# One kernel of attention and token/channel mixing: an earlier load of the second token weight, a third staging buffer, and GpSimd masks for batch 1

## Chip, cores and metric

The kernel runs on one core of a Trainium2 chip. The metric is the device time of one launch in microseconds (us). Engines are named as in the profile: PE (TensorE, matrix products), DVE (VectorE), ACT (ScalarE), POOL (GpSimd), and SP (SyncE, which here only issues DMAs; its rows are marked SPq).

## What is computed

```
scores = q k^T / 8 + min(-(cum_i - cum_j), 0), causal;  cum = cumsum(max(s, 0))
attn   = softmax(scores) v                       8 batches, 8 heads, 576 positions, 64 wide
x      = attn, heads side by side                (8, 576, 512)
u      = x + (relu(x^T w_tok1) w_tok2)^T         w_tok1 576x256, w_tok2 256x576
out    = u + relu(u w_ch1) w_ch2                 w_ch1 512x1536, w_ch2 1536x512
```

All inputs and the output are float32 in device memory; the kernel computes in bf16.

## The kernel before

Work is cut by batch, and inside a batch by "quads" of four heads. One quad is: load k and q (two DMAs of 576 KB, L680), cast them to bf16 (L699 to L703 by POOL, DVE or ACT), transpose them (DVE, L714), scores on PE (L759) in two phases of 16 and 24 matmuls into four psum banks, one exponential a head and phase on ACT (L776), the causal mask, and attention times v on PE (L803, nine matmuls a head, called AV below), then a reciprocal and a normalisation on DVE (L812, L817; ACT L823 for some heads of batch 0). Only two neighbouring blocks of 128 keys are kept for a row of queries; a flag computed at run time sends other inputs to the function `general`, which does not run here. v arrives in chunks of 128 rows (L635) and is multiplied by decay weights (L647, by POOL or DVE) before AV can read it.

The mask is made in one of two ways. Where `pem` is true (all of batch 0, and heads 4 to 7 of batch 1) PE adds a matrix of large negative numbers to the scores: L747 before the scores in batch 0, L769 after them in batch 1. Elsewhere POOL sets the masked half of the exponentials to zero afterwards (L784, `affine_select`), one instruction for the diagonal block of four heads, five a quad: two for the first phase and three for the second.

The token mix of batch 0 (`tok0`) goes by four groups m of two heads: x times w_tok1 (L923, ten matmuls), a transposed copy of x (L936, four), then w_tok2 (L942, two), evicted as uT. `chan0` follows with channel weight 1 (L965, 48 matmuls of 512 columns) and channel weight 2 (L988 and L992). Batches 1 to 7 use `tok` (L1028, L1036, L1053, L1057, and L1083 for a transposition by PE) and `chan` (L1111, L1137).

Weights come in float32 and need a staging buffer until they are cast. w_tok2 is staged in a tile of the ring `x`. The four groups of channel weight 1 and the four of weight 2 are staged in the two halves of the tile `ga` (columns 0 and 1536) and in one of the two tiles `vf`, which later hold v. All DMAs are issued by SP in one order.

The order of all instructions on all engines is not written by hand. Each piece of work is an `op` of `Plan` with its engines, costs and what it reads and writes; `once` lays the ops out by list scheduling (PE, SP and POOL take the lowest `prio` that is ready, the others the longest tail), and `run` repeats this 5 + 60 times with slightly shaken tails and keeps the shortest plan. The kernel is then emitted in that order, and each engine runs its instructions strictly in order. `fills` puts matmuls on zeros (L1264) where the plan leaves PE idle in the first 45 us. `load_op` chains the loads: two loads keep the order in which the code names them, while stores may go between.

The order of the loads is set at the end of the function (L1159 to L1199): k and q of batch 0, v for heads 0 to 3 (five chunks), w_tok1, v for heads 4 to 7 (five chunks), w_tok2, the four groups of channel weight 1, then batch 1 with channel weight 2 between its parts.

Of the kernel before, what the change touches and what calls it, by code (L numbers as in the profile page):

```python
# [9 lines left out]
FP32 = mybir.dt.float32  # L10
# [39 lines left out]
RING = 2048  # L50


class Plan:
# [103 lines left out]
    def run(self, passes=5, search=60):  # L157
        best = None
        self.lengths = []
        rng = random.Random(1)  # L160
        base = None
        for i in range(passes + search):
            self.reset()
            if i >= passes:
                for o in self.ops:
                    o.tail = base[o] + (rng.gauss(0.0, 2.0) if rng.random() < 0.02 else 0.0)
            used = {o: o.tail for o in self.ops} if i else None
            order, length = self.once(i > 0)
            if best is None or length <= best[0]:
                best = (length, [(o, o.start, o.fin, o.eng, o.fn) for o in order],  # L170
                        [(b, b.slot, b.begin, b.end) for o in order for b in o.bufs],
                        {r: list(r.uses) for o in order for b in o.bufs for r in (b.ring,)})
                base = used
            self.lengths.append(round(length, 1))
            if i < passes:
                self.tails(order)
                if base is None:
                    base = {o: o.tail for o in self.ops}
        self.length = best[0]
        for o, o.start, o.fin, o.eng, o.fn in best[1]:  # L180
            pass
        for b, b.slot, b.begin, b.end in best[2]:
            pass
        for r, u in best[3].items():
            r.uses = u
        return [o for o, *_ in best[1]]
# [276 lines left out]
def kernel(  # L463
# [28 lines left out]
    PMASK = 1  # L492
    VUS = 1.05
# [122 lines left out]
    pre = s_sb  # L616
# [22 lines left out]
    def stage_v(b, part=None):  # L639
# [30 lines left out]
        if b:  # L670
            return todo
# [60 lines left out]
    def quad(b, h):  # L732
        np_ = (b * H + h) / 2 if b else -3.0 + h / 8
        kT, qT, E = qkt[(b, h, 0)], qkt[(b, h, 1)], Buf(r_E)
        pem = b < PMASK or b == 1 and h > 0
        for ph, blocks in enumerate(PHASES):
# [13 lines left out]
            if b == 0:  # L750
                P.op({"PE": (mocc, mocc + 0.3, mask)}, reads=["neg"], writes=[(p, 1) for p in ps], prio=(np_, 0),
                     ready=(7.6, 9.3)[ph] if h == 0 else 0.0)

            def mm(ps=ps, cols=cols):
                for (jc, a, z, c0) in cols:
                    for qq in range(DQ):
                        for e in range(HQ):
                            p0 = e * TP
                            nc.tensor.matmul(out=ps[e].t[:, c0 : c0 + z - a],  # L759
                                             lhsT=kT.t[p0 : p0 + TP, jc * 128 : jc * 128 + 128, qq],  # L760
                                             rhs=qT.t[p0 : p0 + TP, a:z, qq],
                                             start=(qq == 0 and b > 0 and (not pem or c0 == 0)),
                                             stop=(qq == DQ - 1 and (not pem or b == 0 and jc == cols[-1][0])),
                                             tile_position=(p0, 0))
                if pem and b:
                    for e in range(HQ):
                        for (jc, a, z, c0) in cols:
                            n = min(128, S - jc * 128)
                            nc.tensor.matmul(out=ps[e].t[:, c0 : c0 + n], lhsT=ident[:, :], rhs=neg[:, 0:n],  # L769
                                             start=False, stop=(jc == cols[-1][0]))  # L770
            occ = (0.06 * len(cols) * HQ if pem and b else 0.0) + 0.15 + DQ * sum(c_pe(z - a)[0] + 0.01 for (_, a, z, _) in cols)
            P.op({"PE": (occ, occ + 0.3, mm)}, reads=[(kT, 0), (qT, 0)] + ([(p, 1) for p in ps] if b == 0 else ["neg"] if pem else []),
# [19 lines left out]
        for hh in range(HQ):  # L792
            pa, rc = Buf(r_sc if b < 2 else r_mx, False), Buf(r_rc, False)
# [372 lines left out]
    stage_v(0, 1)  # L1166
# [5 lines left out]
    load_tok2(Buf(r_x))  # L1172
    sga, sv = Buf(r_ga), Buf(r_vf)
# [3 lines left out]
    load_ch1(sga, 0, 3)  # L1177
    stage_qk(1, 0)
    load_ch2(sga, 1536, 0)
    stage_qk(1, HQ)  # L1180
    load_ch2(sv, 0, 1)
    load_ch2(sga, 0, 2)
    v1 = stage_v(1)
    v1[0]()
    v1[1]()
# [3 lines left out]
    load_ch2(sga, 1536, 3)  # L1189
# [13 lines left out]
    for b in range(B):  # L1203
# [8 lines left out]
    P.op({"DVE": (1.3, 1.6, lambda: nc.vector.tensor_tensor_scan(  # L1212
        out=pre[:, :], data0=one_sb[:, :].to_broadcast([64, S]), data1=wn[:, 0:S], initial=0.0, op0=ALU.mult, op1=ALU.add))},
        reads=["wn", ("sq", 10)], writes=["pre"], prio=50)

    def gaps():
        for i in range(3):
            j = 128 * (i + 1)
            nc.vector.scalar_tensor_tensor(out=gap[:, i : i + 1], in0=wn[:, j + 128 : j + 129], scalar=4.8e-7,
                                           in1=pre[:, j - 1 : j], op0=ALU.mult, op1=ALU.is_lt)  # L1220
        nc.vector.tensor_scalar(out=gap[:, 3:4], in0=cum[:, S - 1 : S], scalar1=160.0, scalar2=None, op0=ALU.is_gt)
        nc.vector.tensor_copy(out=bad[0:64, 0:4], in_=gap[:, :])
# [90 lines left out]
```

## Time and profile before

| what | value |
|---|---|
| median of 6 runs | 291.28 us (290.33 to 292.32) |
| the profiled execution | 291.42 us |
| its span in the profile | 289.7 us, so 1.72 us lie around it |
| granted PE clock, mean | 0.998 |
| PE busy | 278.0 us, 2544 matmuls |
| DVE, ACT, POOL busy | 174.9, 187.3, 91.9 us |

The profile shows one execution. A row of a timeline gives the start in us, the duration of the group in us, the engine, the line, the operation, the tiles (written <- read), the shape and the count; in square brackets stands the idle time of the engine before it and what ended it. The durations of matmuls overlap, so what a run of matmuls costs is read from its start to the start of the next.

### The profile page before, as it was taken

The numbers are of one execution on the slowest core, as the hardware profiler recorded it, in microseconds if no ns is written. First come the engines' busy times: TensorE is split into PE (matmuls) and PEld (weight loads), VectorE is DVE, ScalarE is ACT, GpSimd is POOL, SyncE is SP. The second block draws the span as 40 slices with busy tenths as digits, with TensorE's granted clock in tenths as the row PEclk, the third lists the DMA queues.
The fourth block names the chain that finished last, engine by engine and source line by source line (L and its number), as shares of the span: only waits on it lengthen the run. The fifth ranks groups of instructions, "written<-read, shape, count | busy, mean of one in ns | idle before, by whom it ended". The sixth has DMA issues, their size and how long they took to land.

```text
span 289.7 us, 6564 instructions
## 1 busy us (share of the span) xinstructions
PE 278.0 (96%) x2544; PEld 155.5 (54%) x2574; DVE 174.9 (60%) x333; ACT 187.3 (65%) x354; POOL 91.9 (32%) x143
## 2 busy tenths in 40 slices
PE   8889999998999999999999999999999999999994
PEld 3665455455754545456754545456744545357543
DVE  4963885988999765596359585785245513640022
ACT  3876876998899468986894478857842264018500
POOL 4753022637538417731282104621212102000000
PEclk9999999999999999999999999999999999999999
DMA  7999999998649999899964965951005410170032
GB/s 234 290 290 352 405 303 316 300 276 239 164 130 308 172 339 291 253 202 231 275 158 91 308 214 165 289 146 38 2 0 78 142 38 0 54 147 36 2 106 80
DMA packets 68128, 54.07 MB, mean 187 GB/s; under 512 B 53760, under 2 KB 56640, under 8 KB 68096
## 3 DMA queue, kind: packets, MB, share of 16 engines
q1 hardware_dynamic: 68096, 53.64, 66.1%
q8 instruction: 21, 0.34, 0.6%
q14 instruction: 11, 0.09, 0.1%
HBM read 40.65 MB, written 9.44 MB: 173 GB/s over the span
## 4 chain that ended last, share of the span: by engine, by line
PE 83%; SPq 5%; DMA 5%; DVE 3%; issue 2%; ACT 1%; DVEq 0%; ACTq 0%
PE pmx L1137 29%; PE pmx L1111 27%; PE psc L759 5%; PE pmx L803 5%; SPq L635 4%; PE pmx L1028 4%; PE pmx L965 4%; PE pmx L1053 4%; PE pmx L988 3%; DMA qkf<-in_q_dram 3%; DMA x<-in_moe_w_tok_dram 2%; PE psc L923 1%; DVE qkb L701 1%; PE pmx L1036 1%; SPq L680 1%
## 5 line engine op out<-in xcount | busy, mean ns | idle before, releaser
L776 ACT ACTIVATE E<-psc 128x512 bf16<-128x512 f32 x120 | 63.6, 601 | 26.4 <-PE psc L759 23.8
L784 POOL TENSOR_SCALAR_AFFINE_SELECT E<-E 128x512 bf16<-128x512 bf16 (+1 forms) x65 | 37.8, 609 | 99.7 <-ACT E L776 77.8
L1111 PEld LDWEIGHTS <-wc 128*128 128x128 bf16 x528 | 50.7, 98 | 32.1 <-issue 1.0
L1137 PE MATMUL pmx<-wc,gb 128*128 128x512 bf16 (+1 forms) x244 | 53.8, 369 | 0.5
L1111 PE MATMUL pmx<-uTb,wc 128*128 128x320 bf16 x384 | 54.2, 300 | 0.0
L1117 ACT ACTIVATE gb<-pmx 128x320 bf16<-128x320 f32 x80 | 34.5, 442 | 23.6 <-PE pmx L1111 17.7
L647 POOL TENSOR_TENSOR vp<-vf,wT 128x512 bf16<-128x512 f32 (+2 forms) x35 | 35.2, 1023 | 17.4 <-DMA vf<-in_v_dram 12.2
L685 ACT ACTIVATE junk<-qkf 128x1152 bf16<-128x1152 f32 x32 | 37.5, 1172 | 3.9 <-DMA qkf<-in_k_dram 3.7
L1137 PEld LDWEIGHTS <-gb 128*128 128x128 bf16 x252 | 23.7, 98 | 25.5 <-issue 0.9
L1137 PE MATMUL pmx<-wc,ga 128*128 128x512 bf16 x137 | 32.9, 380 | 0.4
L1111 PE MATMUL pmx<-uTa,wc 128*128 128x512 bf16 x141 | 31.8, 380 | 0.2
L803 PEld LDWEIGHTS <-E 128*128 128x128 bf16 x576 | 20.9, 97 | 6.4 <-issue 2.1
L817 DVE TENSOR_TENSOR x<-pmx,rc 128x320 bf16<-128x320 f32 x48 | 23.1, 489 | 1.4
L1117 ACT ACTIVATE ga<-pmx 128x512 bf16<-128x512 f32 x27 | 16.1, 597 | 11.6 <-PE pmx L1111 11.6
L1145 DVE TENSOR_TENSOR of<-pmx,ub 128x512 f32<-128x512 f32 (+1 forms) x17 | 11.2, 658 | 20.0 <-PE pmx L1137 17.0
L714 DVE STREAM_TRANSPOSE kT<-qkb 128x576 f32<-128x576 f32 x16 | 20.1, 1254 | 3.4 <-PE psc L759 2.3
L1137 PEld LDWEIGHTS <-ga 128*128 128x128 bf16 x144 | 13.1, 98 | 15.5 <-issue 1.5
L759 PE MATMUL psc<-qT,kT 32*128 32x256 bf16 (+2 forms) x592 | 19.1, 251 | 1.9 <-DVE qT L714 1.8
L714 DVE STREAM_TRANSPOSE qT<-qkb 128x576 f32<-128x576 f32 x16 | 19.9, 1244 | 0.4 <-POOL qkb L699 0.3
L701 DVE CAST qkb<-qkf 128x1152 bf16<-128x1152 f32 (+1 forms) x22 | 16.5, 763 | 4.9 <-DMA qkf<-in_k_dram 3.0
L759 PEld LDWEIGHTS <-kT 32*128 32x128 bf16 x640 | 13.7, 92 | 10.3 <-issue 8.1
L812 DVE RECIPROCAL rc<-pmx 128x5 f32<-128x5 f32 x48 | 8.7, 184 | 14.3 <-PE pmx L803 13.7
(115 smaller groups left out, 294.0 us busy)
## 6 DMA issues: line engine op xcount, KB each, us to landing
qkf<-in_k_dram SPq DMA_DIRECT2D x20, 576.0 KB, 6.1
qkf<-in_q_dram SPq DMA_DIRECT2D x20, 576.0 KB, 6.5
out_dram<-of SPq DMA_DIRECT2D x31, 256.0 KB, 2.4
vf<-in_v_dram SPq DMA_DIRECT2D x28, 256.0 KB, 5.9
ga<-in_moe_w_ch_dram SPq DMA_DIRECT2D x6, 768.0 KB, 7.2
vf<-in_v_dram SPq DMA_DIRECT2D x15, 128.0 KB, 5.1
vf<-in_moe_w_ch_dram SPq DMA_DIRECT2D x2, 768.0 KB, 9.9
out_dram<-of SPq DMA_DIRECT2D x10, 128.0 KB, 2.4
```

The costliest lines, as they stand in the source:

```text
L647: eng.tensor_tensor(out=vp.t[0:n, c, h0:h1, 0:D], in0=vf.t[0:n, c, h0:h1, :], in1=wT[0:n, c, b * H + h0 : b * H + h1].unsqueeze(2).to_broa ...
L685: P.op({"ACT": (1.1, 1.5, lambda: nc.scalar.activation(out=junk[:, :], in_=f.t[:, :], func=AF.Square, accum_out=sq[:, col : col + 1]))}, r ...
L701: nc.vector.tensor_copy(out=o.t[:, a:z], in_=i.t[:, a:z])
L714: nc.vector.transpose(out=T.t[:, 0:S, :].rearrange("p s q -> p (s q)").bitcast(FP32).rearrange("p (t r) -> p r t", r=R), in_=t1.t[:, :].bi ...
L759: nc.tensor.matmul(out=ps[e].t[:, c0 : c0 + z - a], lhsT=kT.t[p0 : p0 + TP, jc * 128 : jc * 128 + 128, qq], rhs=qT.t[p0 : p0 + TP, a:z, qq ...
L776: nc.scalar.activation(out=E.t[:, e, ph * 512 : ph * 512 + 512], in_=p.t[:, :], func=AF.Exp, scale=0.125)
L784: nc.gpsimd.affine_select(out=w, in_=w, compare_op=ALU.is_ge, fill=0.0, base=0, pattern=[[0, HQ], [1, n]], channel_multiplier=-1)
L803: nc.tensor.matmul(out=o[:, ic, 0 : D + 1], lhsT=E.t[:, hh, d0 : d0 + 128], rhs=vp.t[:, jc, h + hh, 0 : D + 1], start=(jc == j_lo), stop=( ...
L817: nc.vector.tensor_tensor(out=x.t[:, :, (h + hh) * D : (h + hh + 1) * D], in0=o[:, :, 0:D], in1=rc.t[:, :].unsqueeze(2).to_broadcast([128, ...
L1111: nc.tensor.matmul(out=pm.t[:, 0 : e - a], lhsT=wc1[:, m, cc * 128 : cc * 128 + 128], rhs=uT.t[:, m, a:e], start=(m == 0), stop=(m == NMC ...
L1117: lambda cc=cc, pm=pm, a=a, e=e: nc.scalar.activation(out=g.t[:, cc, a:e], in_=pm.t[:, 0 : e - a], func=AF.Relu),
L1137: nc.tensor.matmul(out=pm.t[:, na:nb], lhsT=g.t[:, cc, c * 128 : c * 128 + 128], rhs=wc2[:, cc, na:nb], start=(cc == 0), stop=(cc == NCC - 1))
```

## The change

1. `Plan.run` searches 100 times instead of 60, and besides the tails it now shakes the priorities of whole groups of PE work (`moved`); a plan that gets stuck is skipped.
2. `pem` holds for batch 0 alone: heads 4 to 7 of batch 1 are masked by POOL (L784) and the block of L769 is gone.
3. `w_tok2` is loaded after the second of the five v chunks for heads 4 to 7 of batch 0, no longer after the fifth.
4. A second tile of the ring `vf` stages channel weights: group 3 of weight 1 goes to it (before: to the first half of `ga`), and the groups of weight 2 take `ga` 0, `ga` 1536, `vf` and `ga` 0. Group 2 of weight 2 is loaded after the first v chunk of batch 1, no longer ahead of all of them.
5. The AV results of heads 4 to 7 of batch 0 go to the psum ring `pmx` instead of `psc`.
6. `pre` is a tile of its own, [64, 3], filled by a reduction over three blocks and two additions instead of a running sum over 576 columns in the tile of `s`.

```diff
-    def run(self, passes=5, search=60):
+    def run(self, passes=5, search=100):
...
             if i >= passes:
+                mode = rng.random()
                 for o in self.ops:
-                    o.tail = base[o] + (rng.gauss(0.0, 2.0) if rng.random() < 0.02 else 0.0)
+                    o.tail = base[o] + (rng.gauss(0.0, 2.0) if mode < 0.7 and rng.random() < 0.02 else 0.0)
+                trial = dict(moved)
+                if mode > 0.4:
+                    for g in sorted({p[0] for p in ranks.values()}):
+                        if rng.random() < 0.1:
+                            trial[g] = trial.get(g, 0.0) + rng.gauss(0.0, 0.7)
+                for o, p in ranks.items():
+                    o.prio = (p[0] + trial.get(p[0], 0.0),) + p[1:]
...
-    pre = s_sb
+    pre = sb("pre", [64, 3], FP32, fast)
...
-        if b:
+        if b or part and LATER:
             return todo
...
-        pem = b < PMASK or b == 1 and h > 0
+        pem = b < PMASK
...
-                if pem and b:
-                    for e in range(HQ):
-                        for (jc, a, z, c0) in cols:
-                            n = min(128, S - jc * 128)
-                            nc.tensor.matmul(out=ps[e].t[:, c0 : c0 + n], lhsT=ident[:, :], rhs=neg[:, 0:n],
-                                             start=False, stop=(jc == cols[-1][0]))
...
-            pa, rc = Buf(r_sc if b < 2 else r_mx, False), Buf(r_rc, False)
+            pa, rc = Buf(r_sc if b == 0 and h == 0 or b == 1 else r_mx, False), Buf(r_rc, False)
...
-    stage_v(0, 1)
+    vh = stage_v(0, 1)
+    vh[0]()
+    vh[1]()
+    load_tok2(Buf(r_x))
+    vh[2]()
+    vh[3]()
+    vh[4]()
     quad(0, HQ)
...
-    load_tok2(Buf(r_x))
-    sga, sv = Buf(r_ga), Buf(r_vf)
+    sga, sv, sv2 = Buf(r_ga), Buf(r_vf), Buf(r_vf)
     load_ch1(sga, 0, 0)
     load_ch1(sga, 1536, 1)
     load_ch1(sv, 0, 2)
-    load_ch1(sga, 0, 3)
+    load_ch1(sv2, 0, 3)
     stage_qk(1, 0)
-    load_ch2(sga, 1536, 0)
+    load_ch2(sga, 0, 0)
     stage_qk(1, HQ)
-    load_ch2(sv, 0, 1)
-    load_ch2(sga, 0, 2)
     v1 = stage_v(1)
+    load_ch2(sga, 1536, 1)
     v1[0]()
+    load_ch2(sv, 0, 2)
     v1[1]()
     v1[2]()
     v1[3]()
     v1[4]()
-    load_ch2(sga, 1536, 3)
+    load_ch2(sga, 0, 3)
...
-    P.op({"DVE": (1.3, 1.6, lambda: nc.vector.tensor_tensor_scan(
-        out=pre[:, :], data0=one_sb[:, :].to_broadcast([64, S]), data1=wn[:, 0:S], initial=0.0, op0=ALU.mult, op1=ALU.add))},
+    P.op({"DVE": (0.5, 0.7, lambda: nc.vector.tensor_reduce(
+        out=pre[:, :], in_=wn[:, 0:384].rearrange("p (c n) -> p c n", n=128), op=ALU.add, axis=mybir.AxisListType.X))},
```

As built, the change reorders every engine, since the plan is drawn anew. On PE 20 matmuls (L769) go and none is added but fills. On POOL five masks are added, the casts of groups 2 and 3 and of half of group 0 of channel weight 1 and of group 1 of weight 2 come to it, and its half of the cast of w_tok2 goes to ACT. On SP no DMA is added or dropped.

## The prediction

> **What bounds the kernel now.** I read the page's shares first, then the chain that ended last, then the PE rows for the places where PE stands still.
>
> ```profile
> PE 278.0 (96%) x2544; PEld 155.5 (54%) x2574; DVE 174.9 (60%) x333; ACT 187.3 (65%) x354; POOL 91.9 (32%) x143
> ...
> PE 83%; SPq 5%; DMA 5%; DVE 3%; issue 2%; ACT 1%; DVEq 0%; ACTq 0%
> ```
>
> PE is the bound: 96% busy and 83% of the chain. The rest of the chain must lie early, because a table of busy time by 20 us gives PE 17.3 to 19.1 us of each 20 up to 80 us, and 19.8 or more in nearly all later ones. So a gain is either PE work that goes, or a place before 80 us where PE waits. These are the places in the timeline of PE:
>
> ```profile
> 18.76 0.68 PE L1264 MATMUL pmx<-zero 128*128 128x512 bf16 x3
> 19.27 1.07 PE L803 MATMUL psc<-vp,E 128*128 128x65 bf16 x27
> 20.18 0.37 PE L1264 MATMUL pmx<-zero 128*128 128x499 bf16 x1
> 21.25 0.59 PE L942 MATMUL psc<-w,h 128*128 128x512 bf16 x2 [0.70 <-POOL w L846]
> ...
> 27.37 0.38 PE L965 MATMUL pmx<-uTa,wc 128*128 128x512 bf16 x1
> ```
> ```profile
> 44.43 0.62 PE L769 MATMUL psc<-neg,ident 128*128 128x128 bf16 x8
> 44.88 2.75 PE L988 MATMUL pmx<-wc,gb 128*128 128x512 bf16 x11
> ...
> 48.14 0.74 PE L769 MATMUL psc<-neg,ident 128*128 128x128 bf16 x12
> 48.71 1.46 PE L988 MATMUL pmx<-wc,gb 128*128 128x512 bf16 x6
> 50.01 1.79 PE L803 MATMUL psc<-vp,E 128*128 128x65 bf16 x45
> 51.95 0.43 PE L803 MATMUL psc<-vp,E 128*128 128x65 bf16 x9 [0.16 <-DVE x L817]
> 52.58 0.43 PE L803 MATMUL psc<-vp,E 128*128 128x65 bf16 x9 [0.20 <-DVE x L817]
> ...
> 68.94 0.64 PE L759 MATMUL psc<-qT,kT 32*128 32x256 bf16 x16 [0.90 <-DVE qT L714]
> ```
>
> Read in them: fills and a wait of 0.70 us at 20 us until w_tok2 is cast; twenty mask matmuls at 44 and 48 us; small waits of the AV of batch 1; 0.90 us for a transposed q at 69 us. The chain names the first wait: w_tok2 is issued at 15.54 us and lands 4.94 us later, at 20.48 us.
>
> ```profile
> 15.54 4.94 DMA x<-in_moe_w_tok_dram
> 20.50 0.67 ACT w L850
> ```
>
> I sum against the profiled execution, 291.42 us (span 289.7 and 1.72 around it); the median of the runs is 0.14 below it, which I neglect.
>
> **Step A: w_tok2 three chunks earlier.** On SP it moves ahead of three v chunks, each of them now one issue later. The weight and the five chunks go through the same queue, so the bytes up to the last of the six are the same, and the last chunk now lands about when the weight did: 20.5 us, against 18.1 us at which DVE began the last three multiplications. So the wait for the weight does not just vanish; the last v chunk is late next. From there: two DVE multiplications of 0.36 us (three took 1.09), AV of heads 4 to 7 from about 21.0 us (27 AV matmuls took 0.91 us from start to start, so 36 take 1.2) to 22.2, w_tok2 for the second group 0.43 to 22.6. Group 3 needs heads 4 and 5 normalised: AV end of head 7, reciprocal 0.18, hand-over 0.2, one normalisation 0.49, at 23.0. Then L923 0.87, L936 0.22, a first L965 0.22 to 24.3; group 4 waits for two more normalisations (0.49 each, 24.0: hidden): 0.87, w_tok2 0.43, L936 and L965 0.44, w_tok2 0.43: 26.5 us with two L965 done. Before, PE stands at 27.37 us with one done. The gain is 0.9 + 0.2 = 1.1 us. It is bounded by the fills and waits that can go at most (0.5 + 0.37 + 0.70 and the 0.28 and 0.31 of idle beside them: about 2.0 us), and on the other side by a last chunk that needs the 5.1 us which chunks took (median) from an issue at 16.15: 21.3 us, and both casts of w_tok2 on ACT in a row (0.67 each, instead of side by side with POOL): a loss of 0.2. I take -1.1 (-2.0 to +0.2).
>
> **Step B: the masks leave PE.** From start to start the eight and the twelve matmuls take 0.45 and 0.57: -1.0 us, on the bounding engine, with nothing beside it.
>
> **Step C: the new wait behind POOL.** Before, the AV of a head of this quad needs only that head's two exponentials. Now it needs the masks, and each mask covers four heads, so the first AV waits for the last exponential and three masks of the second phase. Three masks took 1.59 us at 90 us and 2.27 us at 43 us:
>
> ```profile
> 43.20 2.27 POOL L784 TENSOR_SCALAR_AFFINE_SELECT E<-E 128x256 bf16<-128x256 bf16 x3 [2.31 <-ACT E L776]
> ```
>
> From the end of the score matmuls: 0.3 and four exponentials 2.07, then 1.6 to 2.3 and a hand-over: AV can start 4.2 to 4.9 us later. In the order as built PE has until then: 6 L988 (1.30), the 36 AV of heads 0 to 3 (1.2, the last held by its psum bank until the fourth exponential), 3 L988 (0.65): 3.3 us. That is a wait of 0.9 to 1.6 us; behind it in PE's order stand the last 9 L988 and the whole token mix of batch 1, and the stores of batch 0 wait for those. The old waits here (0.16 + 0.20) go. I take +0.8 net; bounds: -0.4 (POOL just in time) and +1.9 (the normalisations behind it, four of about 0.67 with the reciprocal, exceed the 1.94 us of the nine L988 that should hide them).
>
> The rows of DVE show what runs beside a mask: two L647 took 2.10 us at 43.91 us, where one alone took 0.69 at 42.87 us. [...]
>
> **Step D: the q of batch 2.** The order as built puts 44 instead of 32 L1111 ahead of the scores of heads 4 to 7 of batch 2: 12 x 0.136 = 1.6 us of cover over a wait of 0.90. The wait goes: -0.9 (0 if q lands as late as before and PE is 1.6 us earlier).
>
> **Step E: what is late next.** POOL as built does the cast of k of batch 3 (1.14) and the first v chunk of batch 3 (1.04) before the three masks of the first quad of batch 2. Before, POOL did those masks at 67.83 us and that chunk after them, when it landed:
>
> ```profile
> 67.83 2.10 POOL L784 TENSOR_SCALAR_AFFINE_SELECT E<-E 128x512 bf16<-128x512 bf16 x3
> 70.28 2.15 POOL L647 TENSOR_TENSOR vp<-vf,wT 128x512 bf16<-128x512 f32 x2 [0.36 <-DMA vf<-in_v_dram]
> ```
>
> If the chunk lands at 70.2 as before, the masks end at 70.2 + 1.0 + 1.6 = 72.8; if it comes 1.3 us sooner, at 71.5. PE gets to that AV at 71.15 - 1.3 (A to C) - 0.9 (D) + 1.6 (the twelve L1111) = 70.6. Wait 0.9 to 2.2, less the 0.21 that waits there now. The chunk should come sooner: the DMA queue has a hole now, because group 3 of channel weight 1 waits for its buffer,
>
> ```profile
> 17.26 0.99 SPq L888 DMA_DIRECT2D vf<-in_moe_w_ch_dram  x1
> 23.54 0.37 SPq L888 DMA_DIRECT2D ga<-in_moe_w_ch_dram  x1
> ```
>
> and the third buffer closes it, and the stores of batch 0, which stand ahead in SP's queue, leave earlier. I take +0.7 (-0.2 to +2.0).
>
> **Nothing:** the shorter sum `pre` (1.28 us on DVE at 78 us, which is 60% busy; if that cover were gone, some 0.7 us), the casts moved to POOL (32% busy, idle from 26 to 32 us) and the move of AV to `pmx`. The order of batches 3 to 7 is drawn anew over the same work: 0 (-0.8 to +1.2, by the waits of 0.3 to 0.9 that PE shows here and there now).
>
> Sum: -1.1 - 1.0 + 0.8 - 0.9 + 0.7 = -1.5: **289.9 us**.
>
> **Rivals.**
> - *The chunk takes the place of the weight.* If the last v chunk lands at 21.3 us, A is +0.2 at worst and about 0 by its middle; for it speaks that the six transfers share one full queue, against it the 1.6 us of fills and waits around 20 us. Then 289.9 + 1.1 = 291.0, no measurable change.
> - *GpSimd's own queue sets the pace* (slower). POOL runs in order; if the three masks take 2.3 us and the chunk of batch 3 lands no sooner than 70.2, C is +1.9 and E +2.0, and the following quad's masks, which stand behind two more chunks, cost PE about as much as C again (0.8), with D at 0: -1.1 - 1.0 + 1.9 + 0 + 2.0 + 0.8 = +2.6: 294.0; it decides as soon as C and E together pass 3.0 us. For it: POOL's masks stand behind DMAs. Against it: POOL is idle two thirds of the time, and its masks waited for ACT 77.8 us in all.
> - *Everything stays hidden*: C -0.4 and E 0: 291.42 - 1.1 - 1.0 - 0.4 - 0.9 = 288.0.
>
> **Numbers.** What a measurement can tell from no change is 0.3%, 0.9 us. Forecast (289.0 to 290.5) 0.52, no measurable change 0.26, GpSimd's queue 0.12, everything hidden 0.10. Faster by over 0.3%: 0.52 + 0.10 = 0.62; within: 0.26; slower: 0.12. The range reaches from half of the hidden case to the far side of the no-change case: 288.3 to 291.8.
>
> **What would show it.** A: L965 in a run from 26.5 us, fills gone at 19 to 20 us, AV of heads 4 to 7 starting on a DMA of v. B: no L769. C: a wait of about 1 us of an AV on POOL near 50 us. D: no wait of L759 near 68 us. E: a wait of an AV on POOL near 71 us. The prediction is wrong if the AV at 21 us starts later than 22, if the waits on POOL exceed 3 us, or if PE after 80 us waits more than the 1 to 2 us that it does now.

## The result, and the profile after

The changed kernel takes a median of 294.59 us (289.94 to 298.17), the kernel before on the same chip 291.31; the ratio is 1.0045, with a 95% interval of 1.0028 to 1.0062. The ratio counts 19 of the 37 runs of the changed kernel, those within 1.5% of its fastest, and is smaller than the medians suggest, since 16 of the 18 runs that it leaves out have a mean granted clock of 0.995 or less. The prediction, 289.9 us and faster, was wrong: the kernel became slower, by 1.3 us by the ratio and 3.3 us by the medians, and the median lies above the range. The profiled execution took 293.35 us (span 291.6 and 1.75 around it), 1.93 more than the one of before.

The page after, shares and the row of the granted PE clock:

```profile
PE 279.3 (96%) x2522; PEld 155.1 (53%) x2554; DVE 166.9 (57%) x325; ACT 188.6 (65%) x359; POOL 99.4 (34%) x153
...
PEclk9999999999799999999999999999999999999999
```

PE has 22 records fewer and is yet busy 1.3 us longer. The clock row says why: in the eleventh slice (72.9 to 80.2 us) stands a 7. The timeline of PE, at the places where the prediction had its steps:

```profile
20.37 0.61 PE L955 MATMUL psc<-w,h 128*128 128x512 bf16 x2
20.82 1.25 PE L816 MATMUL pmx<-vp,E 128*128 128x65 bf16 x36
...
26.49 1.89 PE L978 MATMUL pmx<-uTa,wc 128*128 128x512 bf16 x8
```
```profile
48.21 1.40 PE L816 MATMUL psc<-vp,E 128*128 128x65 bf16 x36
50.53 0.81 PE L1001 MATMUL pmx<-wc,gb 128*128 128x512 bf16 x3 [0.92 <-ACT wc L863]
51.18 1.25 PE L816 MATMUL psc<-vp,E 128*128 128x65 bf16 x36
...
54.20 1.89 PE L1041 MATMUL pmx<-x,w 128*128 128x512 bf16 x8
```

In the kernel before, the token mix of batch 1 stood here:

```profile
55.76 1.90 PE L1028 MATMUL pmx<-x,w 128*128 128x512 bf16 x8
```

Up to here it goes as forecast, or better: the run of L978 (L965 before) starts at 26.49 us (forecast 26.5), no mask matmul is left, and the token mix of batch 1 starts at 54.20 instead of 55.76. Only the wait at 50.5 us has another end than the one forecast: not GpSimd's masks, but ACT's cast of group 3 of channel weight 2. Then comes this:

```profile
68.48 0.63 PE L778 MATMUL psc<-qT,kT 32*128 32x256 bf16 x16
...
70.04 1.25 PE L1124 MATMUL pmx<-uTb,wc 128*128 128x320 bf16 x8 [0.28 <-DVE gb L1132]
71.13 0.47 PE L816 MATMUL pmx<-vp,E 128*128 128x65 bf16 x9
73.95 0.83 PE L816 MATMUL pmx<-vp,E 128*128 128x65 bf16 x18 [2.35 <-DVE gb L1132]
```

One wait of 2.35 us, the longest of PE once the kernel has started, not on GpSimd but on DVE, for an eviction (L1132) that frees the psum tile in which AV writes. Here is what DVE has in its queue ahead of that eviction, and, second, what GpSimd does meanwhile:

```profile
69.92 1.22 DVE L733 STREAM_TRANSPOSE qT<-qkb 128x576 f32<-128x576 f32 x1
70.98 0.32 DVE L1239 SCALAR_TENSOR_TENSOR gap<-wn,pre 64x1 f32<-64x1 f32 x1
71.23 0.14 DVE L1238 TENSOR_TENSOR pre<-pre 64x1 f32<-64x1 f32 x1
71.40 0.92 DVE L1239 SCALAR_TENSOR_TENSOR gap<-wn,pre 64x1 f32<-64x1 f32 x1
...
72.43 0.48 DVE L1239 SCALAR_TENSOR_TENSOR gap<-wn,pre 64x1 f32<-64x1 f32 x1
...
73.00 0.50 DVE L1242 COPY bad<-gap 64x4 f32<-64x4 f32 x1
73.42 0.87 DVE L1132 TENSOR_SCALAR gb<-pmx 128x320 bf16<-128x320 f32 x2
```
```profile
70.31 1.00 POOL L797 TENSOR_SCALAR_AFFINE_SELECT E<-E 128x512 bf16<-128x512 bf16 x2
71.27 1.04 POOL L666 TENSOR_TENSOR vp<-vf,wT 128x512 bf16<-128x512 f32 x1
72.27 1.22 POOL L797 TENSOR_SCALAR_AFFINE_SELECT E<-E 128x512 bf16<-128x512 bf16 x2
```

These seven instructions on 64 rows and one to four columns (function `gaps`, the comparisons that follow the sum `pre`) hold DVE for 2.44 us, 70.98 to 73.42. In the kernel before, the comparisons stood at 80.6 us, behind the evictions and ahead of a cast, and PE had no wait there. DVE of the kernel before:

```profile
80.61 1.28 DVE L1219 SCALAR_TENSOR_TENSOR gap<-wn,s_sb 64x1 f32<-64x1 f32 x3
...
81.98 0.16 DVE L1222 COPY bad<-gap 64x4 f32<-64x4 f32 x1
```

The redrawn order has them between a transposition and the eviction. And they are slow where they meet GpSimd: the 0.92 us of one ends at 72.32, just as GpSimd's multiplication ends (72.31); the copy ends at 73.50, just as its masks end (73.49).

Last, the windows of the stretch after the wait (columns: length; busy us and count of PE, weight loads, DVE, ACT, POOL; granted clock; DMA share; GB/s):

```profile
70.00:75.00 5.00, 2.61 (x47) 2.06 (x50) 4.86 (x13) 2.85 (x6) 5.00 (x8) 1.00 0.78 174
75.00:77.50 2.50, 2.50 (x36) 1.73 (x29) 2.36 (x7) 1.03 (x2) 0.50 (x1) 0.54 0.66 194
77.50:80.00 2.50, 2.50 (x16) 1.57 (x14) 1.26 (x1) 1.33 (x4) 0.00 (x0) 0.77 0.01 1
```

PE idles 2.4 of 5 us, and then gets clock 0.54 and 0.77: at half clock (0.50 in each stretch from 75.5 to 78.5 us) for 2.30 + 1.15 = 3.45 us, so up to 1.7 us of PE work is lost (an estimate from these windows). My theory after this (T1): the small operations cost a wait by their place in DVE's queue, they are long because of GpSimd, and the wait costs a second time through the clock. The rivals: T2, GpSimd's masks set this AV and the small operations only stand in the gap; T3, the redrawn order of batches 3 to 7 costs the time.

### The profile page after: what moved, and what is told of

Same layout as the page of the kernel before. It is cut to its first block, busy times and chain, and to the rows that moved or that the text cites. A ratio compares the mean times of both kernels' runs of the same rounds, so it can differ in the third digit from the quotient of the medians.

```text
span 291.6 us, 6540 instructions
## 1 busy us (share of the span) xinstructions
PE 279.3 (96%) x2522; PEld 155.1 (53%) x2554; DVE 166.9 (57%) x325; ACT 188.6 (65%) x359; POOL 99.4 (34%) x153
## 4 chain that ended last, share of the span: by engine, by line
PE 74%; DMA 10%; DVE 7%; ACT 3%; issue 2%; SPq 2%; POOL 0%; DVEq 0%; POOLq 0%
PE pmx L1150 25%; PE pmx L1124 24%; DMA qkf<-in_k_dram 5%; DMA qkf<-in_q_dram 5%; PE pmx L816 5%; PE psc L778 4%; PE pmx L978 4%; PE pmx L1041 4%; PE pmx L1066 3%; ACT E L789 2%; DVE kT L733 2%; DVE qT L733 2%; PE pmx L1001 2%; PE psc L936 1%; PE pmx L1049 1%
## 5 line engine op out<-in xcount | busy, mean ns | idle before, releaser
L797 POOL TENSOR_SCALAR_AFFINE_SELECT E<-E 128x512 bf16<-128x512 bf16 (+1 forms) x70 | 40.5, 606 | 105.4 <-ACT E L789 92.0
L789 ACT ACTIVATE E<-psc 128x512 bf16<-128x512 f32 x120 | 63.5, 602 | 17.1 <-PE psc L778 16.7
L1124 PE MATMUL pmx<-uTb,wc 128*128 128x320 bf16 x384 | 56.5, 304 | 0.8 <-DVE uTb L1106 0.6
L666 POOL TENSOR_TENSOR vp<-vf,wT 128x512 bf16<-128x512 f32 (+2 forms) x36 | 34.8, 980 | 17.1 <-PE pmx L816 8.1
L1124 PE MATMUL pmx<-uTa,wc 128*128 128x512 bf16 x140 | 32.4, 379 | 0.6 <-DVE ga L1132 0.3
L1130 ACT ACTIVATE ga<-pmx 128x512 bf16<-128x512 f32 x31 | 18.5, 597 | 22.3 <-PE pmx L1124 22.2
L830 DVE TENSOR_TENSOR x<-pmx,rc 128x320 bf16<-128x320 f32 x51 | 24.1, 487 | 1.3
L816 PE MATMUL pmx<-vp,E 128*128 128x65 bf16 x468 | 18.7, 194 | 2.4 <-DVE gb L1132 2.4
L1158 DVE TENSOR_TENSOR of<-pmx,ua 128x512 f32<-128x512 f32 x12 | 8.3, 691 | 17.7 <-remote 9.2
```

Source lines behind the costliest of these rows:

```text
L666: eng.tensor_tensor(out=vp.t[0:n, c, h0:h1, 0:D], in0=vf.t[0:n, c, h0:h1, :], in1=wT[0:n, c, b * H + h0 : b * H + h1].unsqueeze(2).to_broa ...
L789: nc.scalar.activation(out=E.t[:, e, ph * 512 : ph * 512 + 512], in_=p.t[:, :], func=AF.Exp, scale=0.125)
L797: nc.gpsimd.affine_select(out=w, in_=w, compare_op=ALU.is_ge, fill=0.0, base=0, pattern=[[0, HQ], [1, n]], channel_multiplier=-1)
L816: nc.tensor.matmul(out=o[:, ic, 0 : D + 1], lhsT=E.t[:, hh, d0 : d0 + 128], rhs=vp.t[:, jc, h + hh, 0 : D + 1], start=(jc == j_lo), stop=( ...
L830: nc.vector.tensor_tensor(out=x.t[:, :, (h + hh) * D : (h + hh + 1) * D], in0=o[:, :, 0:D], in1=rc.t[:, :].unsqueeze(2).to_broadcast([128, ...
L1124: nc.tensor.matmul(out=pm.t[:, 0 : e - a], lhsT=wc1[:, m, cc * 128 : cc * 128 + 128], rhs=uT.t[:, m, a:e], start=(m == 0), stop=(m == NMC ...
```

## The experiments

"Before" is the kernel before on the same chip. The two columns of times are medians of all runs.

| run | this, us | before, us | ratio, 95% interval |
|---|---|---|---|
| e1_gaps_late | 290.62 | 291.08 | 0.9995 (0.9972 to 1.0018) |
| e2_one_sbuf_input | 291.33 | 291.08 | 1.0014 (0.9993 to 1.0035) |
| e3_pe_kept_busy | 292.42 | 291.08 | 1.0056 (1.0027 to 1.0085) |
| e4_before_gaps_early | 294.11 | 291.08 | 1.0100 (1.0065 to 1.0136) |
| e5_masks_on_pe | 291.07 | 290.42 | 1.0011 (0.9987 to 1.0036) |
| e6_wtok2_late | 291.95 | 290.42 | 1.0052 (1.0016 to 1.0088) |
| e7_evict_first | 290.23 | 290.42 | 0.9983 (0.9954 to 1.0011) |
| e8_before_gaps_late | 291.15 | 290.42 | 1.0021 (0.9995 to 1.0047) |
| e9_after_half_w2 | 289.84 | 290.33 | 0.9980 (0.9962 to 0.9998) |
| e10_before_half_w2 | 289.70 | 290.33 | 0.9985 (0.9966 to 1.0003) |
| e11_redrawn | 290.35 | 290.33 | 1.0006 (0.9977 to 1.0034) |
| e12_after_less_dve | 291.47 | 290.85 | 1.0017 (0.9992 to 1.0042) |
| e13_before_less_dve | 290.59 | 290.85 | 0.9997 (0.9970 to 1.0023) |
| e14_after_less_dve_2 | 290.67 | 290.64 | 1.0010 (0.9986 to 1.0033) |
| e15_before_less_dve_2 | 289.75 | 290.64 | 0.9987 (0.9961 to 1.0014) |
| e16_evict_first_2 | 290.77 | 290.69 | 0.9994 (0.9971 to 1.0016) |
| e17_less_dve_evict | 290.42 | 290.69 | 0.9994 (0.9968 to 1.0021) |
| e18_floors_moved | 290.35 | 290.25 | 1.0010 (0.9980 to 1.0041) |

### The small operations: place, length, and the clock

**e1_gaps_late** edits the finished plan of the changed kernel:

```diff
+    late = P.op({"DVE": (0.5, 0.8, gaps)}, reads=["pre", "wn", "cum"], writes=["bad0"], prio=50)
     order = P.run()
+    late.start = 190.0
+    order.sort(key=lambda o: (o.start, o.idx))
```

> The changed kernel with one edit: the seven small VectorE operations that compare the partial sums stand 120 us later in VectorE's queue; nothing else moves. T1 (VectorE's queue holds the eviction that the AV at 74 us waits for, and the clock falls behind that wait): no wait over 0.5 us at 70 to 76 us, the granted clock stays at 1.0 there, and 2.35 + 1.4 us come back less what else is late: 289.6 us (289.2 to 290.2). T2 (GpSimd's masks or the v chunk of batch 3 hold this AV, and the small operations only stand in the gap): the wait of some 2 us stays with another end, the time falls by 0.5 at most: 293 us. T3 (the redrawn order of batches 3 to 7 costs it): time within 0.5 us of the changed kernel.

Measured: 290.62 us, no wait of PE from 70 to 80 us, clock 1.0. The timeline of PE of e1_gaps_late at the place:

```profile
70.54 1.80 PE L1124 MATMUL pmx<-uTb,wc 128*128 128x320 bf16 x12
72.18 1.11 PE L816 MATMUL pmx<-vp,E 128*128 128x65 bf16 x27
73.23 0.64 PE L778 MATMUL psc<-qT,kT 32*128 32x256 bf16 x24
```

All 27 AV matmuls now run without a break, though GpSimd does the same masks and chunks; T2 falls. The order of batches 3 to 7 is the same as in the changed kernel, so T3 falls too. By the medians some 3.7 us come back: 294.59 to 290.62, with the two medians of before 0.23 apart; by the ratios, 1.0045 to 0.9995, it is 1.5. But 290.62 is not the 289.6 expected: against the kernel before, the interval holds no change. Where the rest of the forecast gain is, is the second question below.

**e4_before_gaps_early** is the opposite test: the kernel before, unchanged but for the place of the scan and the comparisons.

```diff
+    moved_pre.start, moved_gaps.start = 64.08, 70.1
+    order.sort(key=lambda o: (o.start, o.idx))
```

> The kernel before with its scan and its comparisons moved forward in VectorE's queue to the place where the changed kernel has them, just ahead of the eviction that the AV of batch 2 waits for; nothing else is changed. T1: the AV near 71 us waits some 2 to 3 us for VectorE, the clock falls in some runs, and the time rises by 2.0 to 3.5 us: 293.4 to 294.9 us. T2 and T3 (place of the small operations costs nothing): 291.4 us as before, within 0.5.

Measured: 294.11 us, +3.0 (+2.9 by the ratio), as T1 has it. PE of e4_before_gaps_early shows the same wait, DVE the same cause (here the comparisons are three instructions, one row):

```profile
73.36 0.43 PE L803 MATMUL pmx<-vp,E 128*128 128x65 bf16 x9 [2.16 <-DVE gb L1119]
```
```profile
70.83 1.48 DVE L1219 SCALAR_TENSOR_TENSOR gap<-wn,s_sb 64x1 f32<-64x1 f32 x3
...
72.42 0.50 DVE L1222 COPY bad<-gap 64x4 f32<-64x4 f32 x1
```

With the place of the scan and the comparisons alone the kernel before becomes as slow as the changed one. The control, the same kernel with them late:

```diff
-    moved_pre.start, moved_gaps.start = 64.08, 70.1
+    moved_pre.start, moved_gaps.start = 189.0, 190.0
```

> Control: the kernel before with its scan and its comparisons 110 us later in VectorE's queue. T1: where the kernel before has them (78 to 82 us) nothing of PE waits behind them, so nothing is gained: 291.1 us within 0.4. Rival (they cost the kernel before something too, so that the changed kernel loses less by them than the comparison with e1_gaps_late says): 290.5 or less.

Measured for e8_before_gaps_late: 291.15 us against 290.42, no gain; by this there is nothing to win where the kernel before had them. (The late place is not quite free either: matched matmul by matmul with the profile of before, e8 is 1.08 us ahead at 192 us and 0.18 at 193.3, behind a wait of PE of 0.73 us for an addition, L1145, that stands behind the moved operations in DVE's queue.)

**e2_one_sbuf_input** leaves them in place and changes their form: the partial sum comes in as a scalar per partition, no longer as a second tensor, the two additions change in the same way, and the copy goes.

```diff
-            nc.vector.scalar_tensor_tensor(out=gap[:, i : i + 1], in0=wn[:, j + 128 : j + 129], scalar=4.8e-7,
-                                           in1=pre[:, i : i + 1], op0=ALU.mult, op1=ALU.is_lt)
-        nc.vector.tensor_copy(out=bad[0:64, 0:4], in_=gap[:, :])
+            nc.vector.tensor_scalar(out=bad[0:64, i : i + 1], in0=wn[:, j + 128 : j + 129], scalar1=4.8e-7,
+                                    scalar2=pre[:, i : i + 1], op0=ALU.mult, op1=ALU.is_lt)
```

> The changed kernel with the small operations where they are, but each with one SBUF tensor input (the partial sum as a scalar per partition) and written straight to its place, without the copy. [...] Rival: each small operation is slow by itself or by the dependence on the one before: block 2.0 us or more, time 293 us.

By T1, with GpSimd as what makes them slow, a block of about 1.0 us (an estimate: six operations at the 0.14 us of L1238 and L1241 in the changed kernel, and gaps), a wait of about 0.9 and a time of 290.3 us (289.8 to 291.5) were expected. Measured: 291.33 us. DVE of e2_one_sbuf_input, then PE:

```profile
71.31 0.16 DVE L1239 TENSOR_SCALAR bad<-wn,pre 64x1 f32<-64x1 f32 x1
71.36 0.18 DVE L1238 TENSOR_SCALAR pre<-pre 64x1 f32<-64x1 f32 x1
71.57 0.20 DVE L1239 TENSOR_SCALAR bad<-wn,pre 64x1 f32<-64x1 f32 x1
...
72.13 0.87 DVE L1132 TENSOR_SCALAR gb<-pmx 128x320 bf16<-128x320 f32 x2
```
```profile
72.65 0.83 PE L816 MATMUL pmx<-vp,E 128*128 128x65 bf16 x18 [0.76 <-DVE gb L1132]
```

The block shrinks from 2.44 to 0.82 us (71.31 to 72.13) and the wait from 2.35 to 0.76, while GpSimd is busy throughout (5.00 of the 5 us from 70 to 75). Each sum still waits for the one before, so it was not this that made them slow. Nor is it the old form by itself: e18_floors_moved, below, has it unchanged at a place where GpSimd is busy for 0.00 us (231 to 233 us). DVE of e18_floors_moved:

```profile
232.28 0.15 DVE L1239 SCALAR_TENSOR_TENSOR gap<-wn,pre 64x1 f32<-64x1 f32 x1
...
232.78 0.16 DVE L1242 COPY bad<-gap 64x4 f32<-64x4 f32 x1
```

So it takes both, the old form and a GpSimd at work: the comparisons took 0.32 to 0.92 us with two tensors beside GpSimd, 0.16 to 0.20 with one, and 0.15 with two and GpSimd idle. It does not strike every instruction of that form: the additions, of two tensors too, took 0.14 us in the changed kernel. The copy goes as the comparisons, 0.50 us beside GpSimd and 0.16 with GpSimd idle. By what GpSimd holds them is not shown.

**e3_pe_kept_busy** keeps the wait and takes away only PE's idleness:

```diff
+    for i in range(10):
+        f = Op()
+        f.start, f.idx = 71.5, 0
+        f.fn = lambda: nc.tensor.matmul(out=r_sc.tiles[3][:, 0:512], lhsT=zero[:, 0:128], rhs=zero[:, 0:512],
+                                        start=True, stop=True)
+        fills.append(f)
```

> The changed kernel with ten matmuls of zeros (512 columns, 2.2 us in all) on PE in front of the AV that waits at 74 us; the wait itself stays, filled. The output is as before. T1 (the half clock from 75.2 us follows PE's idle time): AV starts no sooner, but the granted clock stays at 1.0 from 70 to 80 us and 1.4 us come back: 291.9 us (291.4 to 292.6), with a narrower spread of runs. Rival (the clock falls for a reason that is not this idle time): 293.3 us and a half clock somewhere at 70 to 80 us as before.

Measured: 292.42 us. In e3_pe_kept_busy AV still comes late, but nothing is slow after it:

```profile
72.58 2.32 PE L1292 MATMUL psc<-zero 128*128 128x512 bf16 x9
74.97 0.83 PE L816 MATMUL pmx<-vp,E 128*128 128x65 bf16 x18
75.73 0.64 PE L778 MATMUL psc<-qT,kT 32*128 32x256 bf16 x24
```
```profile
75.00:77.50 2.50, 2.50 (x58) 2.08 (x58) 2.36 (x9) 0.77 (x2) 1.52 (x2) 1.00 0.82 248
77.50:80.00 2.50, 2.50 (x21) 1.78 (x19) 2.46 (x4) 2.18 (x6) 0.00 (x0) 1.00 0.20 41
```

Up to 70 us this execution goes as that of e1_gaps_late; then its scores start 2.50 us later (75.73 against 73.23), and its span is 2.7 longer: that is the wait, paid once. By the medians, and by the ratios, the wait costs 292.42 - 290.62 = 1.8 us. The price of the clock is read best in the two profiles: matched matmul by matmul, the changed kernel is 1.02 us ahead of e3_pe_kept_busy at 76 us and 0.59 behind at 80, so the half clock costs 1.6 us of that execution. By the medians of all runs the changed kernel has 294.59 - 292.42 - 0.23 = 1.9 us on top of e3; the ratios, 1.0045 and 1.0056, do not show it. How often it strikes is seen in the runs: the mean granted clock was 0.995 or less in 20 of 37 runs of the changed kernel (their median 295.23, that of the others 292.68) and in 3 of 8 of e4_before_gaps_early, in none of the 34 of e1, e2 and e3, and in 5 of 179 runs of the kernel before beside the experiments. The spread did narrow, but less than I had hoped (291.05 to 294.96).

### Where is the rest of the forecast gain?

Without step E the forecast was -2.2 us; e1_gaps_late shows -0.15 by its ratio, -0.5 by its medians. First, are the parts real?

**e5_masks_on_pe** undoes step B in e1_gaps_late:

```diff
+        tem = b == 1 and h > 0
...
+                for e in range(HQ if tem else 0):
+                    for (jc, a, z, c0) in cols:
+                        n = min(128, S - jc * 128)
+                        nc.tensor.matmul(out=ps[e].t[:, c0 : c0 + n], lhsT=ident[:, :], rhs=neg[:, 0:n],
+                                         start=False, stop=(jc == cols[-1][0]))
```

> The changed kernel with the small operations late (as in e1_gaps_late), and the masks of heads 4 to 7 of batch 1 back on PE (20 matmuls more on PE, six GpSimd instructions less); order otherwise the same. If step B is worth its busy time, PE is 0.45 + 0.57 = 1.0 us later at 55 us and the end follows by 0.5 to 1.0: 291.1 to 291.6 us against 290.6. Rival (the wait for the cast of channel weight 2 at 50 us, 0.92 us in e1_gaps_late, takes the matmuls in, so that they cost nothing): 290.6, and that wait shrinks to under 0.3.

Measured: 291.07 us, by the ratios 0.5 later than e1_gaps_late, which the intervals do not tell from nothing. PE of e5_masks_on_pe:

```profile
50.86 0.81 PE L1009 MATMUL pmx<-wc,gb 128*128 128x512 bf16 x3 [0.76 <-ACT wc L871]
...
55.54 1.90 PE L1049 MATMUL pmx<-x,w 128*128 128x512 bf16 x8 [0.84 <-DVE x L838]
```

The token mix is 0.96 later (55.54 against 54.58), but that is not the time of the masks on PE: the AV behind the wait at 50.9 us starts at 51.51 us, in e1_gaps_late at 51.55. The rest is a new wait of 0.84 us for a normalisation, behind a cast on DVE that runs beside a cast on GpSimd (51.53 to 52.67 us) and takes twice the 0.75 us of e1_gaps_late. DVE of e5_masks_on_pe:

```profile
51.76 1.53 DVE L720 CAST qkb<-qkf 128x1152 bf16<-128x1152 f32 x1
```

So this run gives no price for step B. And the third group of scores of batch 2 starts at 69.47 (69.98 in e1_gaps_late): by then nothing of the 0.96 is left.

**e6_wtok2_late** undoes the place of the DMA of step A:

```diff
+    at = {o.idx: o for o in order}
+    at[67].start = 16.0
```

> The changed kernel with the small operations late (as in e1_gaps_late), and the DMA of w_tok2 back behind the last v chunk of batch 0 in SP's queue; nothing else moves. If step A holds, w_tok2 lands near 20.5 us, its casts and the first x-times-w_tok products start about 1 us later, channel mix of batch 0 (two done at 25.7 in e1_gaps_late) has two done near 26.7, and the end is 0.5 to 1.1 later: 291.1 to 291.7 us. Rival (later waits on transfers take the gain in): same 26 us mark, end within 0.3 of e1_gaps_late, 290.6.

Measured: 291.95 us, by the ratios 1.7 later than e1_gaps_late. PE waits 1.50 us near 21 us, and the second L978 starts at 27.19 instead of 25.67. Part of the loss may be the clock again (0.993 or less in 4 of 12 runs). Step A is real; but its 1.5 us at 56 us, too, are 0.04 at the third scores of batch 2 (70.02). These scores are a rough mark: over the five profiles of the changed order they start between 68.48 and 70.10 us.

**e7_evict_first** moves the sum `pre` late as well, and one transposition of q behind two evictions:

```diff
+    at[1390].start = 189.0
+    at[167].start = 65.7
```

> The changed kernel with the small operations late (as in e1_gaps_late), the reduction of step Nothing late as well, and one transposition of q (batch 2) behind the two evictions which it holds up near 66 us. T1 (VectorE's queue, in order, is what PE waits for between 60 and 75 us): the 0.56 us wait of PE near 67 us goes, end 0.3 to 0.6 earlier than e1_gaps_late: 290.1 us (289.6 to 290.6). Rival (q of batch 2 comes late from memory and holds PE at the next scores anyway): 290.6 with a wait of the scores near 69 us.

Measured: 290.23 us, the best ratio of the orders that compute everything, and its interval holds no change. The wait near 67 us is gone, as T1 says.

**e9_after_half_w2 and e10_before_half_w2** test whether transfers take the lead back (T4), by the same edit in e1_gaps_late and in the kernel before:

```diff
-                   out=st.rearrange("p (c n) -> p c n", c=CG),
+                   out=st.rearrange("p (c n) -> p c n", c=CG)[:, :, 0 : DM // 2],
```

(and as many columns of the source).

> As e1_gaps_late, but each of the four transfers of channel weight 2 brings only the first half of its columns (this leaves half of the weight unread, so the output is not that of the reference; the work of every engine stays the same). T4 (the transfers between 30 and 70 us, at a share of 1.0, decide when q and k of batch 2 come, and so take back the lead that steps A and B give at 55 us): q and k of batch 2 land 1.5 us or more earlier, the waits at 60 to 70 us go, and the end falls 1.0 to 2.0 us below e1_gaps_late: 288.6 to 289.6 us. Rival (the lead is lost in VectorE's own queue, whatever the transfers do): the landings move, the end stays within 0.5 of e1_gaps_late.

> Control for e9_after_half_w2: the kernel before with the same half transfers of channel weight 2 (half of that weight is not read here either). T4: its wait of 0.90 us at 69 us goes or shrinks, the end falls by 0.5 to 1.0 us to about 290.2; the changed kernel without its small operations in the way is then 1.0 to 1.8 us faster than this one, where with whole transfers it was 0.15. Rival: the distance between the two stays under 0.5 us.

Measured: 289.84 and 289.70 us, ratios 0.9980 and 0.9985. Both gain about 0.5 and the distance does not open: T4, at the size expected, falls. The pair shows one thing more. In e9_after_half_w2 group 3 of channel weight 2 lands at 44.5 us (48.6 in the changed kernel), and the wait at 50.6 us is the same 0.92, because ACT does that cast behind the exponentials of the second phase. ACT of e9_after_half_w2, then its PE:

```profile
47.17 2.06 ACT L789 ACTIVATE E<-psc 128x512 bf16<-128x512 f32 x4 [2.02 <-PE psc L778]
49.10 1.49 ACT L863 CAST wc<-ga 128x1536 bf16<-128x1536 f32 x1
```
```profile
50.64 0.81 PE L1001 MATMUL pmx<-wc,gb 128*128 128x512 bf16 x3 [0.92 <-ACT wc L863]
```

It is ACT's order, not the transfer, that makes the wait of step C.

**e11_redrawn** is e1_gaps_late with another seed:

```diff
-SEED = 1
+SEED = 2
```

> As e1_gaps_late with another seed of the search for the order (2 instead of 1): the same work, the order drawn anew. T3's question, what a redrawn order is worth by itself: within 0.8 us of e1_gaps_late (289.8 to 291.4) if the order of batches 3 to 7 is nearly free; more than 1.5 us away if it is not.

Measured: 290.35 us, 1.0006, within 0.4 us of e1_gaps_late by the ratios. By this one other seed a redrawn order is nearly free by itself, unless it puts something into a queue that PE waits for.

**Four runs with less work on DVE** (T5). e12 and e13 cut the normalisations and additions of batch 1, and clear what stays unwritten:

```diff
+                w = D // 4 if b == 1 else D
                 nc.vector.tensor_tensor(
-                    out=x.t[:, :, (h + hh) * D : (h + hh + 1) * D], in0=o[:, :, 0:D],
+                    out=x.t[:, :, (h + hh) * D : (h + hh) * D + w], in0=o[:, :, 0:w],
...
+    for t in (r_x.tiles[2], r_ub.tiles[0], r_us.tiles[0]):
+        nc.gpsimd.memset(t[:, :, :], 0.0)
```

> As e1_gaps_late, but the normalisations and the additions of the token mix of batch 1 on VectorE handle only a quarter of their columns (the rest of x and u of that batch stays zero, so the output is not that of the reference; number and order of the instructions stay the same, three clears on GpSimd at the start are added). In e1_gaps_late VectorE is busy 9.6 of 10 us from 50 to 60 us. T5 (VectorE's queue from 50 to 63 us takes back the lead that PE has at 47 us): some 4 us less on VectorE, the waits of PE at 54 to 63 us go, and the end falls by 1.0 to 1.6 us, to 289.0 to 289.6. Rival (these waits are worth nothing at the end): within 0.4 of e1_gaps_late, relative to the kernel before on the same chip.

> Control for e12_after_less_dve: the kernel before with the same cut of the normalisations and additions of batch 1 (the rest of x and u of that batch stays zero here too). T5: PE of the kernel before has less lead to lose here; the end falls by 0.3 to 0.8 us, and the changed kernel is then 0.8 to 1.5 us faster than this one, where it was 0.15. Rival: the distance stays under 0.5 us, as it did with half of channel weight 2.

Measured: 291.47 and 290.59 us. The test is spoiled: the clears hold GpSimd until 8.0 us, and the first AV starts at 17.1 and 18.0 us instead of 15.4. With the clears at 33.4 us of the plan:

> As e12_after_less_dve, but the clears stand at 33.4 us of the plan, where GpSimd is idle (33.7 to 38.3 us in e1_gaps_late), so that the start is not held up (again only a quarter of the columns of x and u of batch 1 is computed). T5 (VectorE's queue from 50 to 63 us takes the lead back): start as in e1_gaps_late, the waits of PE at 62 to 67 us go, the end falls by 1.0 to 1.6 us relative to the kernel before: ratio 0.994 to 0.996. Rival: ratio within 0.0015 of the 0.9995 of e1_gaps_late.

> As e13_before_less_dve, with the clears where GpSimd is idle; control for e14_after_less_dve_2 (a quarter of the columns of x and u of batch 1 here too). T5: falls by 0.3 to 0.8 us, ratio 0.997 to 0.999, and the changed kernel is 0.8 us or more faster than this one. Rival: both kernels gain the same, and their distance stays under 0.5 us.

Measured: 290.67 and 289.75 us, ratios 1.0010 and 0.9987. If anything the kernel before gains and the changed one does not; T5, at the size expected, falls. But the trace of e14_after_less_dve_2 shows what may have held it (PE, then DVE):

```profile
70.29 1.25 PE L1126 MATMUL pmx<-uTb,wc 128*128 128x320 bf16 x8 [1.03 <-DVE gb L1134]
```
```profile
68.00 0.76 DVE L720 CAST qkb<-qkf 128x1152 bf16<-128x1152 f32 x1 [2.04 <-DMA qkf<-in_q_dram]
68.67 1.25 DVE L733 STREAM_TRANSPOSE kT<-qkb 128x576 f32<-128x576 f32 x1
69.77 0.47 DVE L1134 TENSOR_SCALAR gb<-pmx 128x320 bf16<-128x320 f32 x1
```

DVE idles 2.04 us in front of a cast whose q is not there, and behind the cast stands the eviction that PE needs. So T6: in the redrawn order a lead of PE ends where an eviction stands behind work that waits for q.

**Three runs on T6.** e16 (from e7) and e17 (from e14) set that eviction ahead of the cast:

```diff
+    at[501].start = 66.8
```

> As e7_evict_first, with one more eviction moved ahead: the single one near 70 us, which stands in VectorE's queue behind a cast that waits for q (it landed at 67.7 us there) and a transposition. T6 (that q's landing, about 68 us whatever lead PE has, is a floor for the eviction behind it, hence for PE): the floor goes, end 0.0 to 0.5 us below e7_evict_first, ratio to before 0.9965 to 0.9983. Rival (PE is at this place no earlier than the eviction): ratio as e7_evict_first, 0.998 within 0.0015.

> As e14_after_less_dve_2 (a quarter of the columns of x and u of batch 1), with the same eviction moved ahead. T6: the wait of 1.03 us of PE at 70.3 us goes, and the end falls by 0.5 to 1.0 us, ratio 0.9975 to 0.9993 where e14_after_less_dve_2 had 1.0010. Rival: the wait moves to the scores of heads 4 to 7 at 72 us (their q), ratio as before.

Measured: 290.77 and 290.42 us, ratios 0.9994 both. In these two the eviction is emitted ahead of the matmuls that fill its tile and takes the tile's older content, so they are no fair test of the order; PE's wait at 70 us goes, but no time is won. Matched matmul by matmul, e17 is 1.35 us further ahead of e14 at 72 us than at 62, and loses 1.4 at 107 us, in a wait of 1.23 for another eviction, behind a transposition that waits 3.27 us for GpSimd's cast of q. e18_floors_moved moves the waiting work back instead, at both places, and the small operations to where DVE idles:

```diff
+    late.start = 234.0
+    at[1390].start = 233.5
+    at[167].start = 65.7
+    at[176].start, at[173].start = 68.85, 68.9
+    at[221].start, at[230].start = 105.2, 108.65
```

> The changed kernel with all the places moved at which VectorE's queue was seen to hold PE: the small operations at 234 us of the plan, where VectorE idles 6.9 us (at 190 us they stand ahead of normalisations that AV near 195 us waits for); the transposition of e7_evict_first; and, near 69 and 106 us, a cast that waits for q from memory, or a transposition that waits for such a cast, placed behind the eviction that it held up. T6 (the redrawn order has evictions behind work that waits for q, so that a lead of PE ends there): no wait of PE on an eviction at 70 and 107 us, a lead of about 1 us at 180 us over e1_gaps_late stays to the end, 1.2 to 1.8 us below the kernel before: ratio 0.994 to 0.996. Rival (the lead ends in the next queue, whatever is moved): ratio 0.998 within 0.0015, as e7_evict_first.

Measured: 290.35 us, 1.0010 (0.9980 to 1.0041). The waits near 107 and 195 us are gone, but there are new ones (the last: GpSimd's masks):

```profile
71.64 0.82 PE L816 MATMUL pmx<-vp,E 128*128 128x65 bf16 x18 [0.75 <-DVE gb L1132]
126.31 0.20 PE L816 MATMUL pmx<-vp,E 128*128 128x65 bf16 x1 [0.35 <-POOL E L797]
```

T6 as a cause that two places explain is not shown: the lead ends in the next queue. None of the versions that compute everything is measurably faster than the kernel before.

## Why the prediction was wrong, step by step

**The step that failed** is the one headed "Nothing": "the shorter sum `pre` (1.28 us on DVE at 78 us, which is 60% busy; if that cover were gone, some 0.7 us)". It took the price of moved small operations from their stage of before and from a mean share of busy time. The change let them move with the order, to the one place in DVE's in-order queue where PE waits for the next instruction, and the order as built, which I had, shows that place. Measured: 2.44 us of DVE's queue and 2.35 of wait for PE, which cost 1.8 us (e3 against e1), and 1.6 us more by the clock in the profiled execution, 1.9 by the medians. The prediction had no term for the clock at all. None of its rivals was this one: the slower side was given to GpSimd's queue, which was on time.

**Step A** (-1.1) held, mechanism included: the last v chunk lands at 20.02 us (20.5 forecast), AV follows it at 20.82 (21.0), the run of L978 starts at 26.49 (26.5), and undoing it costs time. Its size, read at the first scores of batch 1, is 0.9: their mean start is 35.68 in the five profiles of the changed order (the changed kernel, e1, e2, e3, e7) and 36.56 in three of the order before (before, e4, e8).

**Steps B and C** (-1.0 and +0.8): at the token mix of batch 1 the same profiles give 54.50 and 55.57, a lead of 1.1, so B and C together are worth -0.2, which is the sum forecast. In part that is luck. C's wait of 0.92 is ACT's cast, not GpSimd's masks: I had listed what stands behind the masks on PE, and not what the redrawn order puts behind the exponentials on ACT. The cast hides the masks: they are done at 50.79 us, and without its wait PE would have come to that AV at 50.26, so some 0.5 us of wait would have been left (an estimate from these rows). No run gives B and C apart.

**Step D** (-0.9) is the step that is missing even in e1_gaps_late. The wait for q goes from its place, but it was 0.90 only in the profile of before; in e8, which is the same order up to there, it was 0.28, and in e4 0.57. And another hand-over of DVE comes in its stead: 0.56 us for uTb (L1106) near 62.5 us in all five profiles, where the order before has 0.30 for the tile `us` (L1070). At the third scores of batch 2 the means are 69.31 and 68.43 us; with the 12 matmuls more that now stand ahead of them (1.63 us), the lead is 0.75, less than at 55 us, within a spread of 1.6 us in the one order and 0.9 in the other. So D was worth about +0.3, not -0.9.

**Step E** (+0.7): the masks were on time (done at 71.3 us), and with the small operations gone AV does not wait at all. E was 0.

So without the small operations the sum is about -0.9 - 0.2 + 0.3 = -0.8 at 70 us, and -0.15 to -0.5 at the end. What takes the rest is not settled, nor is it shown that anything does: the interval of e1_gaps_late, -0.8 to +0.5 us, still holds the -0.8. Of the causes tried, transfers alone (T4) and DVE's work in one stage (T5) are excluded at the 1 to 2 us expected of them, single evictions behind work that waits for q (T6) are seen to stop PE, and moving two of them only brought out the next.

## What to carry to other kernels

Price a small operation by its place in its engine's queue, not by that engine's busy share: look up in the new order which instruction stands behind it and who waits for that one. When an edit lets a scheduler draw the order anew, read the new order on every engine around each wait of the bounding engine, also for work that the edit only shortens. A gain of a microsecond early in a kernel whose engines run in order is not yet a gain at the end, while a new long wait can be paid twice, as time and as clock (here 1.8 and 1.6 us).

## What the runs showed of the hardware

- **The clock after a wait.** A wait of PE of 2.35 us, with 2.4 of 5 us idle, was followed by 3.45 us at half clock; one of 2.50 us, at 10 us in e13_before_less_dve, by 3.4 us (granted clock 0.62, 0.50, 0.50 and 0.67 in the four us from 11; the mean of that execution is 0.994). In the profile of e4_before_gaps_early a wait of 2.16 us was not (granted clock 1.00 from 72.5 to 85 us). How long a wait it takes is not shown beyond these three.
- **Matmuls on zeros kept the clock.** With 2.3 us of them in the wait (e3_pe_kept_busy) the clock stayed at 1.0, and none of 10 runs had a mean of 0.995 or less.
- **A VectorE instruction on one column can take 0.92 us** beside GpSimd. The same instruction took 0.15 us with GpSimd idle (e18_floors_moved), and 0.16 to 0.20 beside GpSimd with the second tensor passed as a scalar per partition (e2_one_sbuf_input).
